# New operation lengths in the table of a planner that writes every queue

## The chip, the cores and the metric

The kernel runs on one core of one Trainium2 chip. The metric is device microseconds of one execution, from the launch on the device to its end. An execution taken by the profiler gives a span (the first instruction's start to the last one's end) and a time of its own a little above it.

## The reference, cut to what matters

Three stages follow each other. The arrays are float32, the feed-forward weights come as 64-bit floats that are converted on the chip.

```
# 1. attention, 2 batches x 8 heads x 768 positions x 64
bucket(z) = sum((z @ proj > 0) * 2**bit)          # 6 bits
scores = q @ k.T / 8, where bucket(q) == bucket(k), else -1e9
attn = softmax(scores); x = attn @ v              # x: 1536 tokens x 512

# 2. layer 1
h = x @ w_in                                      # 512 -> 2048
x = (h - tanh(h)) @ w_out                         # 2048 -> 512

# 3. layer 2
g = x @ w_gate                                    # 512 -> 1536
out = (g * sigmoid(g) * (x @ w_val)) @ w_out2     # 1536 -> 512
```

## The kernel before, in words

**Attention.** Heads go in pairs, 8 pairs in all, and each pair has 12 steps of 128 query rows (two halves of the sequence, two heads, three tiles). A step is: TensorE scores (L653), VectorE row maximum (L662), ScalarE exponential with row sum (L664), a reciprocal (L668, L670), GpSimd normalisation (L671), six transposes on TensorE (L682), a copy to SBUF (L688). After six steps come the products with the values (L706). For batch 0 GpSimd and ScalarE already split the result into the operands of layer 1 (`x_blocks`, L361 to L368).

**The layers.** Each number is split into a high and a low part, and a product takes three matmuls (high x high, high x low, low x high). The token blocks and the weights are combined after Strassen and Winograd: seven products (L850) instead of eight for a unit, whose sums VectorE forms (`add`, L833) from snapshots that ScalarE took (`snap`, L830). A unit is one of the matrices `in`, `gate` or `val`, 256 of its columns and one batch. Its results go through `block_tanh` (L791), `block_silu` (L798) or `block_val`, that is an activation on ScalarE and a `tt` (L779), and then through `split_g`: rounding on ScalarE (L784) and the remainder in `tt` (L779) again. Then `out_group` multiplies by the output weights (L904). In layer 1 the partial results are copied into a stage (L933) and added to `acc` by a DMA that accumulates, issued on GpSimd (L941), except the first, which is copied (L914, L915), and the last, which VectorE adds (L917). In layer 2 they are added to the output in HBM by such a DMA (L950), the last one by VectorE (L928).

**The weights.** A chunk of 64-bit floats is loaded on SP's queue (L271) into one of two `raw` buffers; three integer steps on VectorE (L273, L276, L279) make 32-bit floats of it in `fs` or `f`; subtractions (L305, L307) form the sums for the seven products, and `split_w` (L285 and L287) or its twin for the output weights (L322, L324) makes high and low parts in `wi` (two buffers) or `wo` (four).

**The planner.** Nothing of the order is written by hand. `op` records each operation with the engines that can do it, its length on each, the keys it reads and writes, a due time and the time `lat` from its end to the moment when others may use it (0.14 by default, 0.25 behind a matmul, some microseconds for a DMA). `Plan.order` then runs a simulation. Whenever an engine is free, it takes the operation with the lowest due time among those that are ready. An operation that names two engines goes to the one that reaches it first; on the second engine its due time is put back by `alt`. Operations that carry `port=BOTH` never overlap in the simulation, whichever of VectorE and GpSimd does them. Lengths of everything but TensorE's work declared behind the attention are multiplied by `SAFE`, 1.05. TensorE's due times are a clock that advances by the length of each product; all other due times are set off against it. The outcome is a list of (operation, engine), and each engine's queue is filled in that order and worked off in that order on the chip, each instruction waiting for its operands' semaphores. So the assumed lengths decide three things: the order in each queue, which engine does the operations that two can do, and when in the simulation a transfer is taken as landed. They don't change what an instruction does.

In the diff `W_TS` is the first integer step of a conversion, `W_STT` the two others; `pool(n)`, `dve(n)` and the new `act(n)` are the lengths of operations on n elements a partition; `TB` is 384 and `DM` 512. Some lengths of the attention are numbers of their own (0.87 for the maximum, 0.9 for the exponential, 0.95 for the normalisation). The split of batch 0 on GpSimd (`on_pool`) uses `pool(n)`.

Of the kernel before, what the change touches and what calls it, by code (L numbers as in the profile page):

```python
# [13 lines left out]
ACTF = mybir.ActivationFunctionType  # L14
# [171 lines left out]
def lsh_attention_moe_kernel(ctx: ExitStack, tc: tile.TileContext, qT, kT, vP, proj, cst, wts, out):  # L186
# [61 lines left out]
    W_TS, W_STT = 0.43, 0.69  # L248
# [3 lines left out]
    def pool(n):  # L252
        return 0.16 + n / 457

    def dve(n):
        return (n + 151) / 960 - 0.01
# [26 lines left out]
    def split_w(dst, src, rk, wk, n, due, late=False):  # L283
        hi, lo = dst
        op({"ACT": 0.19 + n / 1175}, lambda e: e.activation(out=hi, in_=src, func=ACTF.Copy),  # L285
# [32 lines left out]
    def declare_out(name, f, due, after):  # L318
# [3 lines left out]
        op({"ACT": 0.63}, lambda e: e.activation(out=hi, in_=f_t, func=ACTF.Copy),  # L322
# [455 lines left out]
    def tt(dst, dk, a, ak, b, bk, alu, due, port):  # L778
        op({"DVE": dve(TB), "POOL": pool(TB)} if port else {"DVE": 0.56}, lambda e: e.tensor_tensor(out=dst, in0=a, in1=b, op=alu),  # L779
           r=[ak, bk], w=dk, due=due, alt=ALT, port=BOTH * port)  # L780

    def split_g(key, src, sk, due, psum):
        (hi, hk, h1), (lo, lk, l1) = g_slot(), g_slot()
        op({"ACT": 0.52}, lambda g: g.activation(out=hi, in_=src, func=ACTF.Copy), r=[sk], w=[hk] + h1, due=due)  # L784
# [4 lines left out]
    def block_tanh(key, src, sk, due, psum, keep, spare=None):  # L789
        t, tk, t1 = spare or t_slot(1)  # L790
        op({"ACT": 0.51}, lambda e: e.activation(out=t, in_=src, func=ACTF.Tanh), r=[sk], w=[tk] + t1, due=due)  # L791
# [4 lines left out]
    def block_silu(key, src, sk, due, psum, keep, spare=None):  # L796
        t, tk, t1 = t_slot(2)
        op({"ACT": 0.51}, lambda e: e.activation(out=t, in_=src, func=ACTF.Sigmoid), r=[sk], w=[tk] + t1, due=due)  # L798
# [19 lines left out]
    def products(name, i, sb):  # L818
# [10 lines left out]
        def snap(dst, dk, bank, bk, due):  # L829
            op({"ACT": 0.49}, lambda e: e.activation(out=dst, in_=bank, func=ACTF.Copy), r=[bk], w=dk, due=due)  # L830

        def add(dst, dk, bank, bk, c, ck, due):
            op({"DVE": 0.56}, lambda e: e.tensor_tensor(out=dst, in0=bank, in1=c, op=ALU.add), r=[bk, ck], w=[dk], due=due)  # L833
# [48 lines left out]
    def out_group(layer, i, sb, j):  # L882
# [28 lines left out]
        if layer == 1 and i in (0, NP1 - 1):  # L911
            if i == 0:
                op({"DVE": dve(TB), "ACT": 0.5}, lambda g:
                   g.activation(out=acc_at(sb, j), in_=ps, func=ACTF.Copy) if g is nc.scalar else  # L914
                   g.tensor_copy(acc_at(sb, j), ps), r=[k], w=[("acc", sb, j)], due=e, late=True)  # L915
            else:
                op({"DVE": 0.57}, lambda g: g.tensor_tensor(  # L917
# [12 lines left out]
        else:  # L930
            at_, key, first = stage(layer, m)
            op({"ACT": 0.18 + size / 1200, "DVE": dve(size)}, lambda g, at_=at_:
# [4 lines left out]
            if m == n - 1:  # L937
                at_ = stages[layer, "at"]
                keys = [key[:3] + (c,) for c in range(n)]
                if layer == 1:  # L940
                    op({"POOL": 1.0}, lambda g, at_=at_: g.dma_start(out=acc_at(sb, 4 * t, 4), in_=at_(4), accum_op=ALU.add),  # L941
                       r=keys + aks, w=aks, due=e + 1, lat=5.0, late=True)
                else:
# [5 lines left out]
                    else:  # L949
                        op({"POOL": 1.0}, lambda g, at_=at_: g.dma_start(out=o, in_=src(at_), accum_op=ALU.add),  # L950
                           r=keys + [ok], w=[ok], due=e + 1, lat=5.0)
# [129 lines left out]
```

## Time and profile before

| what | value |
|---|---|
| median of 3 runs | 804.79 us (803.57 to 805.9) |
| the profiled execution | 803.86 us |
| its span | 802.1 us |
| instructions | 12309 |
| TensorE matmul, busy | 766.6 us, 96% |
| VectorE, busy | 589.4 us, 73% |
| ScalarE, busy | 466.8 us, 58% |
| GpSimd, busy | 359.7 us, 45% |

All times are microseconds unless ns is said. PE is TensorE's matmul, PEld its loading of weights, DVE is VectorE, ACT ScalarE, POOL GpSimd, SP the queue engine; L779 is line 779 of the kernel. A line says which engine does which operation, what it writes and reads (out<-in), the shapes, and x how many. An instruction's duration reaches from its start to the acknowledgement of its last write, and the next one on the same engine can start before that, so the sum of busy times counts such overlaps once. Matmul ends are modelled. The attention runs to about 264 us, layer 1 to about 532, layer 2 from there, overlapping at the seams.

### The profile page before, as it was taken

What the parts mean: (1) busy time and instruction counts of PE and PEld (TensorE: products, weight loads), DVE (VectorE), ACT (ScalarE), POOL (GpSimd) and SP (SyncE); (2) the same over time, 40 slices, a digit from 0 to 9 for tenths busy, and PEclk for the clock granted to TensorE, in tenths of its full rate; (3) what the DMA queues carried; (4) which work ended last, traced back from release to release, by engine and by line L of the source; (5) the groups of instructions that cost most, each with busy time, mean ns of one, the idle gap of its engine ahead of it and who ended that gap; (6) DMA issues with size and microseconds to landing.
All of it is one profiled execution on the core that took longest, in us unless ns stands there. A gap on an engine that the chain in (4) does not pass through costs nothing.

```text
span 802.1 us, 12309 instructions
## 1 busy us (share of the span) xinstructions
PE 766.6 (96%) x4332; PEld 661.5 (82%) x4332; DVE 589.4 (73%) x1038; ACT 466.8 (58%) x906; POOL 359.7 (45%) x384
## 2 busy tenths in 40 slices
PE   5999999999999999999999999989989999999997
PEld 3766666666668889999999999989979898989996
DVE  6877777787698966786777668777765876877444
ACT  4787787786666754666545545554544455555530
POOL 4655567744475341343323454735245532344121
PEclk9999999999999999999999999999999999999999
DMA  7655444553222143777776761324327567666675
GB/s 213 161 131 139 109 133 115 124 134 74 73 66 93 53 117 94 165 189 177 178 171 161 157 142 47 86 79 158 120 73 149 128 150 158 121 155 132 119 167 187
DMA packets 38717, 104.23 MB, mean 130 GB/s; under 512 B 4704, under 2 KB 10080, under 8 KB 38656
## 3 DMA queue, kind: packets, MB, share of 16 engines
q1 hardware_dynamic: 28288, 71.06, 29.0%
q0 software_dynamic: 9904, 31.59, 22.9%
q10 hardware_dynamic: 464, 0.80, 0.4%
q8 instruction: 34, 0.56, 0.3%
q14 instruction: 27, 0.22, 0.1%
HBM read 49.17 MB, written 18.87 MB: 85 GB/s over the span
## 4 chain that ended last, share of the span: by engine, by line
PE 76%; DVE 11%; DMA 4%; ACT 3%; issue 3%; POOL 2%; SPq 0%; DVEq 0%; ACTq 0%; POOLq 0%
PE s L850 26%; PE t L904 13%; PE x L706 7%; PE t L682 7%; PE s L653 7%; PE h L904 6%; PE x L904 4%; DMA raw<-in_w 3%; DVE m L662 2%; PE x L850 2%; PE t L850 1%; ACT ct L664 1%; DMA acc<-ct 1%; DVE ct L779 1%; DVE op L779 1%
## 5 line engine op out<-in xcount | busy, mean ns | idle before, releaser
L850 PE MATMUL s<-x,wi 128*128 128x384 f32 x1200 | 235.1, 337 | 6.4 <-DVE ct L833 2.1
L850 PEld LDWEIGHTS s<-x,wi 128*128 128x128 f32 x1200 | 209.1, 188 | 18.6 <-DVE ct L833 4.0
L662 DVE TENSOR_REDUCE m<-s 128x1 f32<-128x768 f32 x96 | 89.3, 951 | 29.3 <-PE s L653 28.7
L671 POOL TENSOR_SCALAR ct<-ct,r 128x768 f32<-128x768 f32 x96 | 94.1, 988 | 33.4 <-DVE r L670 29.2
L664 ACT ACTIVATE ct<-s,m 128x768 f32<-128x768 f32 x96 | 85.8, 896 | 20.6 <-DVE m L662 19.7
L653 PE MATMUL s<-op 128*128 128x384 f32 x384 | 88.9, 366 | 6.7 <-ACT ct L664 6.4
L830 ACT ACTIVATE ct<-s 128x384 f32<-128x384 f32 x120 | 58.1, 490 | 58.6 <-PE s L850 58.1
L682 PEld LDWEIGHTS t<-csb,ct 128*128 128x128 f32 x576 | 64.4, 141 | 31.2 <-issue 18.7
L682 PE MATMUL t<-csb,ct 128*128 128x128 f32 x576 | 81.6, 278 | 5.2 <-POOL ct L671 1.7
L904 PE MATMUL t<-op,wo 128*128 128x384 f32 x384 | 77.0, 338 | 4.8 <-DVE acc L917 1.5
L653 PEld LDWEIGHTS s<-op 128*128 128x128 f32 x384 | 66.5, 195 | 17.5 <-ACT ct L664 15.3
L904 PEld LDWEIGHTS t<-op,wo 128*128 128x128 f32 x384 | 66.9, 188 | 7.8 <-DVE acc L917 2.1
L706 PE MATMUL x<-pt,v 128*64 128x384 f32 x384 | 69.0, 495 | 0.0
L287 POOL TENSOR_TENSOR wi<-fs,wi 128x512 fp32r<-128x512 f32 (+1 forms) x37 | 57.1, 1553 | 24.1 <-ACT wi L285 18.0
L904 PE MATMUL t<-wo,op 128*128 128x512 f32 x264 | 67.5, 393 | 0.0
L688 ACT ACTIVATE pt<-t 128x768 f32<-128x768 f32 x59 | 47.9, 811 | 29.7 <-PE t L682 28.6
L324 POOL TENSOR_TENSOR wo<-f,wo 128x512 fp32r<-128x512 f32 x17 | 22.4, 1316 | 75.1 <-ACT wo L322 70.9
L904 PEld LDWEIGHTS t<-wo,op 128*128 128x128 f32 x264 | 48.9, 188 | 8.2
L850 PE MATMUL s<-op,wi 128*128 128x384 f32 x240 | 48.2, 337 | 1.8 <-DVE ct L779 1.6
L706 PEld LDWEIGHTS x<-pt,v 128*64 128x64 f32 x384 | 24.7, 136 | 28.4 <-issue 28.4
L285 ACT ACTIVATE wi<-fs 128x512 fp32r<-128x512 f32 (+1 forms) x60 | 41.5, 701 | 10.4 <-DVE fs L305 4.0
L779 POOL TENSOR_TENSOR ct<-ct 128x384 f32<-128x384 f32 x20 | 20.6, 1029 | 59.9 <-ACT ct L791 31.0
(164 smaller groups left out, 1378.8 us busy)
## 6 DMA issues: line engine op xcount, KB each, us to landing
raw<-in_w SPq DMA_DIRECT2D x68, 512.0 KB, 3.9
acc<-ct POOLq DMA_DIRECT2D x24, 768.0 KB, 6.0
out<-acc POOLq DMA_DIRECT2D x16, 768.0 KB, 7.8
op<-raw SPq DMA_DIRECT2D x42, 192.0 KB, 3.0
op<-f SPq DMA_DIRECT2D x56, 96.0 KB, 2.5
v<-in_v SPq DMA_DIRECT2D x8, 384.0 KB, 3.2
out<-acc SPq DMA_DIRECT2D x4, 768.0 KB, 4.1
acc<-out SPq DMA_DIRECT2D x4, 768.0 KB, 4.5
```

The costliest lines, as they stand in the source:

```text
L285: op({"ACT": 0.19 + n / 1175}, lambda e: e.activation(out=hi, in_=src, func=ACTF.Copy), r=rk, w=[wk + (0,)], due=due, late=late)
L287: op({"POOL": pool(n), "DVE": dve(n)}, lambda e: e.tensor_tensor(out=lo, in0=src, in1=hi.bitcast(F32), op=ALU.subtract), r=rk + [wk + (0,) ...
L653: g.matmul(out=s[:, kh, 0:TB], lhsT=(b, a)[first][:, q0], rhs=ks[kh][0 if first else 1], start=first, stop=not first,)
L662: op({"DVE": 0.87}, lambda g: g.tensor_reduce(out=m, in_=sv, axis=AX.XY, op=ALU.max, negate=True), r=[sk + (0,), sk + (1,)], w=[mk], due=d ...
L664: op({"ACT": 0.9}, lambda g: g.activation(out=p.rearrange("p (a b) -> p a b", a=2), in_=sv, func=ACTF.Exp, bias=m, accum_out=sm), r=[sk + ...
L671: op({"POOL": 0.95}, lambda g: g.tensor_scalar(out=p, in0=p, scalar1=r, scalar2=1.0, op0=ALU.mult, op1=ALU.mult), r=[pk, rk], w=[pk], due= ...
L682: g.transpose(out=t_t[0][:, kt // 3, c0:c0 + 128], in_=p[:, kt * 128:(kt + 1) * 128], identity=ident)
L688: op({"ACT": 0.75, "DVE": 0.87}, lambda g: g.activation(out=dst, in_=src, func=ACTF.Copy) if g is nc.scalar else g.tensor_copy(dst, src), ...
L706: g.matmul(out=x[r, :], lhsT=v[:, kt, r], rhs=pt_t[ptks[e][1]][:, kt, :], start=(kt == 0), stop=(kt == NKT - 1), tile_position=(0, 64 * e),)
L830: op({"ACT": 0.49}, lambda e: e.activation(out=dst, in_=bank, func=ACTF.Copy), r=[bk], w=dk, due=due)
L850: e.matmul(out=bank, lhsT=w[:, wpart, wi * 256 + k * 128:wi * 256 + k * 128 + 128], rhs=x_at(sb, xn, xpart, k), start=first and m == 0, st ...
L904: e.matmul(out=ps, lhsT=lhs, rhs=rhs, start=c == 0, stop=c == 5)
```

## The change

All lengths of the list below get new values; `act(n)` is a new function, and nothing else is different. The same formulas at 384 and 512 elements: `dve` 0.547 and 0.681 become 0.468 and 0.601, `pool` 1.000 and 1.280 become 0.970 and 1.250, the ScalarE lengths of 0.49 to 0.52 become 0.39 to 0.42 and 0.626 becomes 0.497. The accumulating DMA of layer 1 has an issue of 0.87 instead of 1.0 and lands 6.0 after it instead of 5.0; that of layer 2 1.3 and 7.5 instead of 1.0 and 5.0.

```diff
...
-    W_TS, W_STT = 0.43, 0.69
+    W_TS, W_STT = 0.34, 0.6
...
     def pool(n):
-        return 0.16 + n / 457
+        return 0.13 + n / 457
...
     def dve(n):
-        return (n + 151) / 960 - 0.01
+        return (n + 65) / 960
+
+    def act(n):
+        return 0.07 + n / 1200
...
     def convert(c, dst, dk, due, after, parts=1):
...
     def split_w(dst, src, rk, wk, n, due, late=False):
...
-        op({"ACT": 0.19 + n / 1175}, lambda e: e.activation(out=hi, in_=src, func=ACTF.Copy),
+        op({"ACT": act(n)}, lambda e: e.activation(out=hi, in_=src, func=ACTF.Copy),
...
-        op({"ACT": 0.63}, lambda e: e.activation(out=hi, in_=f_t, func=ACTF.Copy),
+        op({"ACT": act(512)}, lambda e: e.activation(out=hi, in_=f_t, func=ACTF.Copy),
...
     def tt(dst, dk, a, ak, b, bk, alu, due, port):
-        op({"DVE": dve(TB), "POOL": pool(TB)} if port else {"DVE": 0.56}, lambda e: e.tensor_tensor(out=dst, in0=a, in1=b, op=alu),
+        op({"DVE": dve(TB), "POOL": pool(TB)} if port else {"DVE": dve(TB) + 0.01}, lambda e: e.tensor_tensor(out=dst, in0=a, in1=b, op=alu),
...
     def split_g(key, src, sk, due, psum):
...
-        op({"ACT": 0.52}, lambda g: g.activation(out=hi, in_=src, func=ACTF.Copy), r=[sk], w=[hk] + h1, due=due)
+        op({"ACT": act(TB) + 0.03}, lambda g: g.activation(out=hi, in_=src, func=ACTF.Copy), r=[sk], w=[hk] + h1, due=due)
...
     def block_tanh(key, src, sk, due, psum, keep, spare=None):
...
-        op({"ACT": 0.51}, lambda e: e.activation(out=t, in_=src, func=ACTF.Tanh), r=[sk], w=[tk] + t1, due=due)
+        op({"ACT": act(TB) + 0.02}, lambda e: e.activation(out=t, in_=src, func=ACTF.Tanh), r=[sk], w=[tk] + t1, due=due)
...
     def block_silu(key, src, sk, due, psum, keep, spare=None):
...
-        op({"ACT": 0.51}, lambda e: e.activation(out=t, in_=src, func=ACTF.Sigmoid), r=[sk], w=[tk] + t1, due=due)
+        op({"ACT": act(TB) + 0.02}, lambda e: e.activation(out=t, in_=src, func=ACTF.Sigmoid), r=[sk], w=[tk] + t1, due=due)
...
         def snap(dst, dk, bank, bk, due):
-            op({"ACT": 0.49}, lambda e: e.activation(out=dst, in_=bank, func=ACTF.Copy), r=[bk], w=dk, due=due)
+            op({"ACT": act(TB)}, lambda e: e.activation(out=dst, in_=bank, func=ACTF.Copy), r=[bk], w=dk, due=due)
...
         def add(dst, dk, bank, bk, c, ck, due):
-            op({"DVE": 0.56}, lambda e: e.tensor_tensor(out=dst, in0=bank, in1=c, op=ALU.add), r=[bk, ck], w=[dk], due=due)
+            op({"DVE": dve(TB) + 0.01}, lambda e: e.tensor_tensor(out=dst, in0=bank, in1=c, op=ALU.add), r=[bk, ck], w=[dk], due=due)
...
         def product(n):
...
-                op({"DVE": dve(TB), "ACT": 0.5}, lambda g:
+                op({"DVE": dve(TB), "ACT": act(TB)}, lambda g:
...
-                op({"DVE": 0.57}, lambda g: g.tensor_tensor(
+                op({"DVE": dve(TB)}, lambda g: g.tensor_tensor(
...
-            op({"ACT": 0.18 + size / 1200, "DVE": dve(size)}, lambda g, at_=at_:
+            op({"ACT": act(size), "DVE": dve(size)}, lambda g, at_=at_:
...
-                    op({"POOL": 1.0}, lambda g, at_=at_: g.dma_start(out=acc_at(sb, 4 * t, 4), in_=at_(4), accum_op=ALU.add),
-                       r=keys + aks, w=aks, due=e + 1, lat=5.0, late=True)
+                    op({"POOL": 0.87}, lambda g, at_=at_: g.dma_start(out=acc_at(sb, 4 * t, 4), in_=at_(4), accum_op=ALU.add),
+                       r=keys + aks, w=aks, due=e + 1, lat=6.0, late=True)
...
-                        op({"POOL": 1.0}, lambda g, at_=at_: g.dma_start(out=o, in_=src(at_), accum_op=ALU.add),
-                           r=keys + [ok], w=[ok], due=e + 1, lat=5.0)
+                        op({"POOL": 1.3}, lambda g, at_=at_: g.dma_start(out=o, in_=src(at_), accum_op=ALU.add),
+                           r=keys + [ok], w=[ok], due=e + 1, lat=7.5)
```

## Rows read from the trace of the kernel before

**Rows 1.** The page's chain that ended last, shares of the span by engine.

```profile
PE 76%; DVE 11%; DMA 4%; ACT 3%; issue 3%; POOL 2%; SPq 0%; DVEq 0%; ACTq 0%; POOLq 0%
```

**Rows 2.** Busy us (x instructions) by stage: PE, PEld, DVE, ACT, POOL, clock, DMA share, GB/s.

```profile
264.00:300.00 36.00, 33.63 (x187) 31.88 (x186) 29.70 (x47) 23.09 (x46) 14.84 (x13) 1.00 0.29 75
300.00:460.00 160.00, 159.09 (x903) 155.95 (x903) 117.66 (x211) 89.73 (x190) 54.26 (x51) 1.00 0.68 162
460.00:532.00 72.00, 67.27 (x375) 64.36 (x374) 51.06 (x88) 38.05 (x72) 41.18 (x29) 1.00 0.37 87
532.00:640.00 108.00, 103.90 (x540) 95.09 (x540) 79.24 (x143) 52.56 (x103) 48.47 (x41) 1.00 0.45 125
640.00:782.00 142.00, 141.47 (x736) 130.07 (x735) 96.82 (x171) 71.60 (x139) 45.65 (x40) 1.00 0.68 142
250.00:802.00 552.00, 535.20 (x2883) 500.69 (x2881) 395.15 (x689) 284.72 (x570) 211.88 (x179) 1.00 0.56 134
```

**Rows 3.** PE's waits, 264 to 782 us: us in total, times, longest; twelve rows.

```profile
PE s L850 <- DVE op L779: 2.1, 3, 1.3
...
PE t L904 <- DVE acc L917: 1.5, 2, 1.1
...
PE s L850 <- DVE x L363: 0.2, 1, 0.2
```

**Rows 4.** VectorE's timeline in layer 1: start, duration, line, operation.

```profile
336.19 0.42 DVE L273 TENSOR_SCALAR fs<-raw 128x512 uint32<-128x512 uint32 x1
336.53 0.55 DVE L779 TENSOR_TENSOR op<-s,op 128x384 fp32r<-128x384 f32 x1
336.99 0.68 DVE L276 SCALAR_TENSOR_TENSOR f<-raw,f 128x512 uint32<-128x512 uint32 x1
337.59 0.68 DVE L276 SCALAR_TENSOR_TENSOR fs<-raw,fs 128x512 uint32<-128x512 uint32 x1
```

**Rows 5.** ScalarE's timeline at the passage to layer 2.

```profile
502.38 0.49 ACT L933 ACTIVATE ct<-x 128x384 f32<-128x384 f32 x1 [0.17 <-PE x L904]
502.76 0.49 ACT L791 ACTIVATE ct<-s 128x384 f32<-128x384 f32 x1
```

**Rows 6.** Groups on GpSimd, 250 to 802 us: busy us, mean ns, idle before.

```profile
L950 POOL DMA_DIRECT2D out<-acc x16 | 21.0, 1316 | 35.1 <-ACT acc L933 24.6 <-PE s L850 8.1 <-ACT op L784 2.4
L941 POOL DMA_DIRECT2D acc<-ct x24 | 21.0, 875 | 36.5 <-ACT op L784 11.7 <-ACT ct L933 10.8 <-DVE fs L279 5.8
L779 POOL TENSOR_TENSOR ct<-ct 128x384 f32<-128x384 f32 x20 | 20.6, 1029 | 59.9 <-ACT ct L791 31.0 <-ACT ct L798 26.5 <-DVE ct L833 2.4
```

**Rows 7.** The chain of waits in order of time, 490 to 626 us: start, duration, what.

```profile
498.08 6.72 DMA acc<-ct
...
525.00 0.50 ACT ct L830
525.53 0.58 DVE s L833
...
614.98 7.49 DMA raw<-in_w
```

**Rows 8.** The page's DMA issues: count, KB each, median us to landing.

```profile
acc<-ct POOLq DMA_DIRECT2D x24, 768.0 KB, 6.0
out<-acc POOLq DMA_DIRECT2D x16, 768.0 KB, 7.8
```

**Rows 9.** VectorE's timeline in layer 2, with the idle time before.

```profile
622.49 0.43 DVE L273 TENSOR_SCALAR fs<-raw 128x512 uint32<-128x512 uint32 x1 [3.55 <-DMA raw<-in_w]
```

**Rows 10.** Groups by line and shape on GpSimd in the attention, 25 to 216 us.

```profile
L363 POOL TENSOR_TENSOR x<-ct,x 128x384 fp32r<-128x384 f32 x14 | 14.0, 1002 | 4.1 <-ACT x L361 4.1
...
L368 POOL TENSOR_TENSOR ct<-ct 128x384 f32<-128x384 f32 x8 | 8.1, 1012 | 0.2
```

**Rows 11.** The timeline of all engines around 512 us.

```profile
511.78 2.29 POOL L363 TENSOR_TENSOR op<-acc,op 128x768 fp32r<-128x768 f32 x1
...
512.29 2.06 DVE L273 TENSOR_SCALAR f<-raw 128x512 uint32<-128x512 uint32 x1
```

## The prediction, made before the changed kernel ran

> **What bounds the kernel now.** I read the chain of waits first. Three quarters of the span hang on TensorE and a tenth on VectorE [rows 1]: the end is set by TensorE's own work plus the moments when it stands. So I went to the busy time by stage. After the attention, TensorE is busy 33.63 of 36.00 us, 159.09 of 160.00, 67.27 of 72.00, 103.90 of 108.00 and 141.47 of 142.00 [rows 2]. The differences are 2.4, 0.9, 4.7, 4.1 and 0.5, together 12.6 us between 264 and 782 us. The reader is to see that in the long steady stretches of both layers TensorE never stands; what it loses lies at the start of layer 1, at the passage to layer 2 and in the first fifth of layer 2. VectorE, ScalarE and GpSimd are busy 395, 285 and 212 of 552 us there, so none is a bound by volume. The list of TensorE's waits in that stretch has twelve groups, 21 waits, from 2.1 us down to 0.2 [rows 3]; the large ones are on VectorE. Its clock is at 1.00, the 2.4 GHz level, in every stage, so the clock has no part in it.
>
> TensorE's work itself is untouched by the change, so about 12.6 us is the whole sum that a better order behind the attention can give, and the profiled execution (803.86 us, its span 802.1 with 1.8 around it) is what I count from. The median of the runs shown is 804.79, 0.9 above it.
>
> **What the change edits.** No instruction, size or transfer of the computation is added or removed. The planner simulates the engines and writes down the order of every queue and, for an operation that two engines can do, which one does it. The edit alters only the lengths that it assumes. Are the new ones nearer to the chip?
>
> VectorE: the operation behind a 384-wide one starts 0.46 us after it although that one lasts 0.55 (336.53 to 336.99) [rows 4]. Old length 0.547 (the `dve` formula at 384) or 0.56, new 0.468 or 0.478. The two integer steps of the weight conversion have 0.34 and 0.60 to the next start while lasting 0.42 and 0.68 [rows 4]; old 0.43 and 0.69, new 0.34 and 0.60. ScalarE: 0.38 apart, lasting 0.49 [rows 5]; old 0.49 to 0.52, new 0.39 to 0.42. GpSimd's length falls by 0.03 everywhere. So the old lengths were durations and the new ones are distances, right within 0.01 us; the planner multiplies both by 1.05.
>
> One rule speaks against this. The Trainium skill, "VectorE: DVE Perf Modes", section The DRAIN you can't avoid, says that the next operation does not start until the pipe of the one before it is empty, which would make the duration the distance. By it each VectorE operation would come 0.55 - 0.49 = 0.06 us later than planned, three in a chain, before 21 waits: 3.8 us slower, 807.7. The trace disagrees: the next start lies 0.08 to 0.09 us before the end [rows 4], and the measurement decides.
>
> *What it sums to in the planner.* 689 VectorE operations behind 250 us [rows 2] times 0.083 (0.079 x 1.05) is 57 us less booked in 552; 570 ScalarE operations times some 0.11 is 63 us less. None of this is time of the chip: the operations take what they took. It acts in two ways.
>
> (1) Who does the shared operations. GpSimd does 179 instructions in that stretch [rows 2], of which 24 and 16 issue accumulating DMAs [rows 6]; the other 139 are operations that VectorE could do. One of them takes 1.03 us on GpSimd [rows 6] against 0.55 on VectorE, so each that lies in a chain on which TensorE waits gives back about 0.5 us. VectorE looks 57 us freer to the planner, so it will take some: I take 30 of the 139 (57 us would hold 120 at 0.47; most are taken by whichever engine is free first, and GpSimd stays free half of the time). In chains that end in a TensorE wait I expect one in five of these: 6 x 0.5 = 3 us.
>
> (2) The order on TensorE, VectorE and ScalarE. A step which the planner believes late is placed later than need be; with truer lengths the two layer boundaries (2.4 + 4.7 us of standing) should be packed a little better. But a longer assumed length is also a cushion. The dependent chain of one block is six operations, three on ScalarE and three on VectorE (snapshot, add, tanh, subtract, rounding, remainder): 3 x 0.105 + 3 x 0.083 = 0.56 us less cushion per chain. Is there any left? From the chain: the ScalarE step of 0.50 us from 525.00, and 0.03 later VectorE's, of 0.58 [rows 7]: 0.53 and some 0.61 from start to start. The planner now says 0.39 x 1.05 + 0.14 = 0.55 and 0.478 x 1.05 + 0.14 = 0.64. Both still cover the rows by 0.03, so nothing undisturbed arrives late. Bounds for the whole of (1) and (2): all 12.6 us gone below; above, all 21 waits longer by 0.56, 11.8 us. The value that I take is a third of the standing at the boundaries and in the first part of layer 2, (2.4 + 4.7 + 4.1) / 3 = 3.7 us, which contains the 3 us of (1); nearest to the rows that show undisturbed chains still covered.
>
> **The DMA edits.** Accumulating into `acc` lands after 6.0 us (old 5, new 6), accumulating into `out` after 7.8 (old 5, new 7.5) [rows 8], and their issues hold GpSimd for 0.88 and 1.32 us [rows 6] (old 1.0 both, new 0.87 and 1.3). Nobody is queued behind them long: the only TensorE chain with a landing of `acc` in it is the one at the passage to layer 2, where it stands with 6.72 us from 498.08 [rows 7]. Gain between 0 and 1.1 us, the longest of TensorE's waits on `acc` [rows 3]; I take 0, as it is in the third above. The weight stream's landing stays at 3.5 us in the planner, and one load took 7.49 [rows 7]; VectorE stood 3.55 us before its conversion [rows 9]. The change does not mend this, and those waits stay.
>
> **The attention.** Its lengths stay, except that the 384-wide GpSimd operations that split its result go from 1.00 to 0.97; there are 22 of them, lasting 1.00 to 1.01 [rows 10]. It shifts the simulated clock of GpSimd by 0.03 at a time and can swap neighbours. Bounds -2 and +2 us: two of these of a microsecond swapped either way in the final stretch, where the weights of layer 1 are already being converted. I take 0, since these rows fit either length.
>
> Sum: 803.86 - 3.7 = 800.2 from the profiled execution; the median lies 0.9 above, 801.1. I say 801.
>
> **Rivals.** *A, no change (804.8, the median as it is).* TensorE's order is fixed by due times whenever its operands are ready, and in 302 us of steady stretches they are ready [rows 2]. If the waits at the boundaries come from the dependence itself, with the products of the first block needing the split of a whole half, other lengths only shift them. For it: the waits are spread over twelve small groups. Against: the shared operations will really change hands. That the edit does nothing to the order at all would end here as well; with some 120 us of booked time changed that is unlikely.
>
> *B, slower (about 809).* Collisions of VectorE and GpSimd. Place: VectorE's queue where GpSimd works at its side. A conversion step that takes 0.42 us took 2.06, ending 0.3 us behind GpSimd's 2.29 us subtraction [rows 11]: the one stood until the other was through. The planner keeps the two apart by booking their shared port for the planned length, so the surplus of 0.08 us behind each VectorE operation was a guard against the chip running off the plan. With only 5% left, any lateness (a weight load at 7.49 for 3.5 us) puts operations side by side. Price: 2.06 - 0.42 = 1.6 us each. It decides the sign when more than 3.7 / 1.6, that is three, new collisions fall into chains that TensorE waits for; four of them with half of the gain lost give 804.8 - 1.9 + 6.4 = 809.3, six give 812.5. For it: the waits stand where GpSimd is busiest, 41 of 72 us at the passage [rows 2]. Against: fewer operations on GpSimd mean fewer partners to collide with. The Trainium skill, "SBUF — State Buffer", Who interferes with whom, states the same as a rule: a VectorE operation that uses the port pair it shares with GpSimd (two inputs in SBUF, or a 2-port mode) and a GpSimd one exclude each other for a whole instruction. By it, a planner that misjudges starts pays whole operations, as in this rival; the trace agrees with its 2.06.
>
> *C, much faster (about 796).* Two thirds of the standing goes, 8.4 us from 804.8, because the passage to layer 2 is mended by the 6.0 us landing. For it: one wait of that passage hangs on `acc`; against: the rest there do not.
>
> **How the numbers follow.** Chances: forecast 0.41, C 0.07, A 0.27, B 0.25. About 0.3%, 2.4 us, is what a measurement of this kernel can tell from no change; faster means below 802.4, slower above 807.2. The forecast's own range is 797 to 803.5, a little of it within no change, which A's upper edge gives back: faster 0.47, same 0.29, slower 0.24. Range: 795 takes in two thirds of C, and 810 takes in B up to four collisions; left out are a third of C and about half of B, 0.15 together. The bounds of (1) and (2), 12.6 either way, lie beyond both ends and are reached only if every wait goes or grows.
>
> **What would show it.** Right: GpSimd's instructions behind 250 us fall from 179 by some 30 and VectorE's 689 rise by as many; TensorE's waits from 264 to 782 us sum to about 9 us, with the passage from 460 to 532 below 4; the attention ends within 2 us of 264. The steady stretches stay at under 1 us each. Rival B: new VectorE operations of two microseconds beside GpSimd ones, and TensorE waits on VectorE above 12.6. The prediction is wrong if the attention's end moves by more than 2 us, since I gave that nothing, or if the steady stretches begin to show waits.

## The result, and the profile after

The changed kernel took 810.55 us (median of 4 runs, 810.01 to 811.53) beside 804.18 of the kernel before on the same chip: a ratio of 1.0080, 95% interval 1.0056 to 1.0105. It is slower by 6.4 us, where 801.0 was predicted. Its profiled execution took 810.85, with a span of 809.1. In its code, lines behind L259 are numbered 3 higher: L850 is L853, L779 L782, L830 L833, L833 L836, L784 L787, L904 L907.

The distances that the change copied into the planner are still those of the chip. VectorE's timeline in layer 1 answers to [rows 4]:

```profile
342.32 0.55 DVE L836 TENSOR_TENSOR ct<-s,ct 128x384 f32<-128x384 f32 x1
342.78 0.68 DVE L279 SCALAR_TENSOR_TENSOR f<-raw,f 128x512 uint32<-128x512 uint32 x1
...
343.94 0.42 DVE L276 TENSOR_SCALAR fs<-raw 128x512 uint32<-128x512 uint32 x1
344.27 0.68 DVE L282 SCALAR_TENSOR_TENSOR f<-raw,f 128x512 uint32<-128x512 uint32 x1
344.87 0.56 DVE L836 TENSOR_TENSOR t<-t,ct 128x384 f32<-128x384 f32 x1
```

A 384-wide operation is followed after 0.46 us, the integer steps after 0.33 and 0.60. So the new table describes these distances better, and the kernel is slower. The landings of the accumulating DMAs, which the table now has at 6.0 and 7.5, did not move either [rows 8]:

```profile
acc<-ct POOLq DMA_DIRECT2D x24, 768.0 KB, 6.0
out<-acc POOLq DMA_DIRECT2D x16, 768.0 KB, 7.7
```

The busy time by stage answers to [rows 2], with the same columns:

```profile
264.00:300.00 36.00, 34.30 (x190) 31.06 (x188) 28.22 (x45) 23.77 (x48) 18.14 (x15) 1.00 0.24 67
300.00:460.00 160.00, 158.13 (x890) 153.44 (x889) 117.79 (x214) 88.21 (x189) 43.66 (x43) 1.00 0.68 162
460.00:532.00 72.00, 69.98 (x392) 67.24 (x390) 57.77 (x95) 40.00 (x76) 37.02 (x28) 1.00 0.41 99
532.00:640.00 108.00, 102.28 (x525) 92.56 (x526) 84.03 (x148) 55.96 (x109) 36.08 (x32) 1.00 0.45 129
640.00:782.00 142.00, 139.51 (x722) 127.52 (x721) 92.81 (x168) 71.11 (x138) 38.77 (x31) 1.00 0.61 123
...
250.00:809.00 559.00, 540.34 (x2895) 502.00 (x2893) 408.06 (x713) 288.91 (x578) 176.74 (x149) 1.00 0.54 131
```

GpSimd has 149 instructions behind 250 us where it had 179, and VectorE 713 where it had 689; GpSimd's loss of 30 is the predicted number, but it is a balance (see the steps of the prediction below). TensorE stands 1.7, 1.9, 2.0, 5.7 and 2.5 us in the stages, together 13.8 where it was 12.6. The passage and the start of layer 2 improved a little (7.7 for 8.8), the steady stretches of both layers got worse (4.4 for 1.4). Two waits head the list from 264 to 782 us, in the columns of [rows 3], and both are steps of a block on a bank of `s`:

```profile
PE s L853 <- ACT op L787: 3.9, 4, 1.4
PE s L853 <- DVE ct L782: 2.5, 4, 0.9
```

The first, on ScalarE's rounding, is new. The second stood in the list before with 1.9:

```profile
PE s L850 <- DVE ct L779: 1.9, 4, 0.7
```

Busy time hides part of the standing, which the prediction did not see. A matmul's end is modelled: a 384-wide one is drawn 0.33 us long, while the next can start 0.173 us after it, so a pause of 0.1 us between two of them still counts as busy. Starts show it: two 384-wide matmuls in a row start 0.173 us apart, 512-wide ones 0.231. What goes beyond that from 270 us to the end, counting pauses over 0.03 us, adds up to 22.4 us in 77 pauses before and 25.4 in 101 after. I use this sum below.

### The profile page after: what moved, and what is told of

It reads as the page before. It is cut to its first block, busy times and chain, and to the rows that moved or that the text cites. A ratio compares the mean times of both kernels' runs of the same rounds, so it can differ in the third digit from the quotient of the medians.

```text
span 809.1 us, 12324 instructions
## 1 busy us (share of the span) xinstructions
PE 770.0 (95%) x4332; PEld 661.1 (82%) x4332; DVE 602.7 (74%) x1067; ACT 468.5 (58%) x911; POOL 322.2 (40%) x350
## 5 line engine op out<-in xcount | busy, mean ns | idle before, releaser
L853 PE MATMUL s<-x,wi 128*128 128x384 f32 x1200 | 236.2, 338 | 7.9 <-ACT op L787 3.9
L853 PEld LDWEIGHTS s<-x,wi 128*128 128x128 f32 x1200 | 208.9, 188 | 21.4 <-ACT op L787 7.7
L674 POOL TENSOR_SCALAR ct<-ct,r 128x768 f32<-128x768 f32 x96 | 92.2, 968 | 32.5 <-DVE r L673 28.5
L667 ACT ACTIVATE ct<-s,m 128x768 f32<-128x768 f32 x96 | 85.9, 897 | 22.9 <-DVE m L665 16.4
L833 ACT ACTIVATE ct<-s 128x384 f32<-128x384 f32 x120 | 58.9, 491 | 48.8 <-PE s L853 46.3
L907 PE MATMUL t<-op,wo 128*128 128x384 f32 x384 | 78.1, 339 | 3.9 <-DVE op L782 1.6
L907 PEld LDWEIGHTS t<-op,wo 128*128 128x128 f32 x384 | 66.6, 188 | 8.5 <-DVE op L782 2.9
L907 PE MATMUL t<-wo,op 128*128 128x512 f32 x264 | 67.8, 393 | 0.0
L691 ACT ACTIVATE pt<-t 128x768 f32<-128x768 f32 x57 | 46.2, 811 | 28.9 <-PE t L685 27.8
L290 POOL TENSOR_TENSOR wi<-fs,wi 128x512 fp32r<-128x512 f32 (+1 forms) x26 | 40.3, 1552 | 46.3 <-ACT wi L288 46.3
L907 PEld LDWEIGHTS t<-wo,op 128*128 128x128 f32 x264 | 48.9, 187 | 7.9
L782 POOL TENSOR_TENSOR ct<-ct 128x384 f32<-128x384 f32 x19 | 20.0, 1052 | 86.2 <-ACT ct L801 47.8
L853 PE MATMUL s<-op,wi 128*128 128x384 f32 x240 | 48.4, 336 | 1.3 <-DVE ct L782 1.0
L944 POOL DMA_DIRECT2D acc<-ct x24 | 21.0, 877 | 67.4 <-ACT ct L936 38.2
```

The costliest lines, as they stand in the source:

```text
L290: op({"POOL": pool(n), "DVE": dve(n)}, lambda e: e.tensor_tensor(out=lo, in0=src, in1=hi.bitcast(F32), op=ALU.subtract), r=rk + [wk + (0,) ...
L667: op({"ACT": 0.9}, lambda g: g.activation(out=p.rearrange("p (a b) -> p a b", a=2), in_=sv, func=ACTF.Exp, bias=m, accum_out=sm), r=[sk + ...
L674: op({"POOL": 0.95}, lambda g: g.tensor_scalar(out=p, in0=p, scalar1=r, scalar2=1.0, op0=ALU.mult, op1=ALU.mult), r=[pk, rk], w=[pk], due= ...
L691: op({"ACT": 0.75, "DVE": 0.87}, lambda g: g.activation(out=dst, in_=src, func=ACTF.Copy) if g is nc.scalar else g.tensor_copy(dst, src), ...
L833: op({"ACT": act(TB)}, lambda e: e.activation(out=dst, in_=bank, func=ACTF.Copy), r=[bk], w=dk, due=due)
L853: e.matmul(out=bank, lhsT=w[:, wpart, wi * 256 + k * 128:wi * 256 + k * 128 + 128], rhs=x_at(sb, xn, xpart, k), start=first and m == 0, st ...
```

## What stood behind the late steps

The largest single wait of that new group, in the timeline of the changed kernel (start, duration, engine, line, operation, and the idle time before with what ended it):

```profile
528.59 2.24 PE L853 MATMUL s<-x,wi 128*128 128x384 f32 x12
...
529.39 0.48 ACT L833 ACTIVATE ct<-s 128x384 f32<-128x384 f32 x1
530.93 0.57 DVE L836 TENSOR_TENSOR s<-s,ct 128x384 f32<-128x384 f32 x1 [1.41 <-PE s L853]
531.54 0.57 DVE L782 TENSOR_TENSOR s<-s,ct 128x384 f32<-128x384 f32 x1
532.14 0.56 DVE L836 TENSOR_TENSOR ct<-s,ct 128x384 f32<-128x384 f32 x1
532.73 0.49 ACT L787 ACTIVATE op<-s 128x384 fp32r<-128x384 f32 x1 [2.86 <-DVE ct L836]
533.27 1.34 PE L853 MATMUL s<-x,wi 128*128 128x384 f32 x6 [1.40 <-ACT op L787]
```

The first row is two products. VectorE's `add` needs the first, which ends at 529.79, and ScalarE's snapshot, through at 529.87. It starts at 530.93, behind the second product (through at 530.83), whose result goes to the other bank of the same tile `s` and is none of its operands. Four steps later TensorE stands for 1.40 us.

`s` is two tiles and `t` one, each of two PSUM banks ([128, 2, 512] float32); `x` and `h` are tiles of one bank. The program's waits are kept by tile: an operation on one bank waits for whatever another engine does on the other bank, if that stands earlier in the program. The planner's keys are single banks, so it does not know these waits. I compared each operation of VectorE and ScalarE behind 264 us with the end of its operands and of its predecessor. Before, 61 start more than 0.3 us late, 65.2 us in all, and 53 of them (60.3 us) end with a matmul on the sibling bank; after, 32 of 41 (37.3 of 43.5 us). The typical one costs 1.08 us, about one product (six matmuls, 1.04 us from start to start). Of TensorE's own standing 7.0 of 12.7 us before and 7.5 of 13.7 after end with an operation on the sibling bank. By the sum of late starts the changed kernel waits less (43.5 us for 65.2), and yet it is slower: what such a wait costs depends on whether TensorE comes to stand behind it, which the sum does not tell.

## The experiments

Texts on record speak of theories by number or letter. *1*: with shorter lengths, a block's chain of dependent steps has less cushion. *1b* (later *H*): the old surplus stood in for time that engines are held by waits which the planner does not know. *2*: who does the shared operations, or the engine's booking, matters. *3* (later *R*): any other order costs a few us by chance. *W*: the waits between banks are the cost. *T*: the attention's end, which comes later, is what is left of the loss. All ratios are to the kernel before on the same chip; differences between runs that stood on different chips are taken from the ratios, at 803.3 us.

**Parts of the change, and the cushion.** On the changed kernel, a chain latency of 0.23 behind the attention; on the kernel before, 0.05:

```diff
-        self.ops.append((eng, fn, deps, due, self.LAT if lat is None else lat, late, after,
+        self.ops.append((eng, fn, deps, due, (self.LAT if not self.n_first else 0.23) if lat is None else lat, late, after,
```

> The changed kernel, with one more edit: behind the attention the planner takes a result as usable 0.23 us after the operation's end instead of 0.14, so a chain of dependent operations is as long in the plan as before the change (0.083 to 0.105 us an operation), while the engines are still booked by the new distances. Theory 1 (the old lengths held a cushion for results that come later than planned, and the change took it away): most of the 6.4 us comes back, 804 to 807 us, and TensorE's waits from 300 to 782 us fall to those of before. Theory 2 (what counts is how long the engines are booked, and through it who does the shared operations): no change from the changed kernel, 810 to 811. Theory 3 (any reshuffling of these queues moves the time by some us, without a rule): anywhere from 803 to 813.

> The kernel before with 0.05 instead of 0.14 us from an operation's end to its use, behind the attention: chains as short in the plan as after the change, engines booked as long as before. Theory 1b: 802 to 806 us. Theory 1: 808 to 812. Theory 3: 804 to 817.

Measured: 809.16 us, 1.0081 (1.0065 to 1.0096), and 806.81, 1.0044 (1.0030 to 1.0058). Giving the chain its 0.09 us a step back mends nothing; taking as much from the kernel before costs 3.5 us.

Then the kernel before with only VectorE's lines of the diff, only ScalarE's, only those of the accumulating DMAs, and those with `pool(n)`:

> The kernel before with VectorE's new lengths alone (dve(n), the two conversion lengths and the fixed VectorE lengths). Theory 1: about half of the chain's cushion is gone (3 of 6 operations), so about half of the loss: 806 to 808 us. Theory 2: nearly the whole loss, 809 to 811, since this part alone lets VectorE take the shared operations from GpSimd. Theory 3: 803 to 813.

> The kernel before with ScalarE's new lengths alone. Theory 1: the other half of the loss, 806 to 808 us. Theory 2: no loss, 804 us, since ScalarE shares few operations with GpSimd. Theory 3: 803 to 813.

> The kernel before with the new issue lengths and landings of the accumulating DMAs alone. It moves 144 operations to another engine and changes the order of as many pairs on VectorE as ScalarE's new lengths alone did (about 600), without making an engine's work shorter. Theory 1b: 802 to 806 us, as before. Theory 3: as b_act, 809 to 817.

> The kernel before with GpSimd's length shorter by 0.03 and the new issue lengths and landings of the accumulating DMAs, nothing else. Theories 1 and 2: the time of before within 0.3%, 802 to 806.5 us, since neither a cushion nor a share moves. Theory 3: the queues are reshuffled here too, so 801 to 810, and if it comes out over 807 the loss has no rule that the lengths explain.

Measured: 817.69, 1.0184 (1.0166 to 1.0202); 813.35, 1.0129 (1.0114 to 1.0144); 806.86, 1.0045 (1.0029 to 1.0061); 803.41, 1.0000 (0.9989 to 1.0012). Shorter lengths of either engine alone cost more than both together, so the parts don't add; an order that is new without shorter lengths on these engines costs 0 or 3.6 us.

Then the changed kernel with its lengths on VectorE and ScalarE booked longer than by 1.05:

```diff
-        eng = {e: t * (1 if e == "PE" or not self.n_first else self.SAFE) for e, t in eng.items()}
+        eng = {e: t * (1 if e == "PE" or not self.n_first else 1.2 if e in ("DVE", "ACT") else self.SAFE) for e, t in eng.items()}
```

> The same with 1.12, half way. Theory 1b: between the two, 805 to 809 us. Theory 3: no order in the three factors; 803 to 817.

> The changed kernel with the lengths of VectorE and ScalarE behind the attention multiplied by 1.20 instead of 1.05: the new table, but engines booked about as long as before the change (384-wide: 0.56 on VectorE, 0.47 on ScalarE). After the first four runs theory 1 is restated as 1b: the booked length stands in for time in which an engine is blocked by waits that the planner doesn't know, not for the latency of a chain. Theory 1b: 802 to 806 us. Theory 1 (latency of a chain): 802 to 806 too. Theory 3 (any reshuffling of the tuned queues costs): about 810, within 804 to 817.

Measured: at 1.12 812.83, 1.0124 (1.0101 to 1.0147); at 1.20 803.60, 1.0006 (0.9992 to 1.0020). At 1.20 the old surplus is back and so is the old time. It is no smooth curve: 1.12 is worse than 1.05, where theory 1b expected 805 to 809; theory 3, that the order of the three factors says nothing, had this right.

**The waits between banks taken out.** The order stays, instruction for instruction; operations on different banks of `s` or `t` are declared independent when they are issued, unless they also share an operand:

```diff
+    def emit(n, e):
+        made.clear()
+        plan.ops[n][1](eng[e])
+        mine = plan.touch[n]
...
+                    for n2, e2, both, i2 in seen.get(other, []):
+                        if e2 != e and not both and n2 not in plan.ops[n][2]:
+                            for i in made:
+                                tc.declare_no_dep(i.ins, i2, reason="another bank")
...
-            plan.ops[n][1](eng[e])
+            emit(n, e)
```

> The changed kernel, in its own order, instruction for instruction, but an operation on one PSUM bank of the tiles s and t no longer waits for a matmul or an operation on the other bank of the same tile (no data pass between the two banks; every wait on the operation's own bank stays). In the trace of the changed kernel 32 of 41 late starts of VectorE and ScalarE behind 264 us (37.3 of 43.5 us) end with such a matmul, and 17 of 27 standings of TensorE (7.5 of 13.7 us) with such an operation. Theory H (the old lengths were too long by about as much as these waits hold the engines up, so they stood in for waits that the planner does not know, and the true lengths are too short only because of them): with the waits gone the true lengths are enough, 797 to 803 us, and no slower than the kernel before with the same waits taken out. Theory R (any other order of some thousand operations costs a few us by chance): it gains at most the 7.5 us of TensorE's standing, to 803 to 810, and stays about 6 us behind the kernel before with the waits taken out.

> The kernel before, in its own order, with the same waits between the two banks of s and t taken out: its trace has 53 of 61 late starts of VectorE and ScalarE behind 264 us (60.3 of 65.2 us) and 15 of 24 standings of TensorE (7.0 of 12.7 us) that end with them. Theory H: the old lengths already leave room for these waits, so most of the 60 us cost nothing and only TensorE's own standing goes, 797 to 803 us, equal to or above the changed kernel without the waits. Theory R: the same 7 us, 797 to 799, and the changed kernel without the waits about 6 us above it.

Measured: the changed kernel 786.78, 0.9795 (0.9782 to 0.9809); the kernel before 785.21, 0.9776 (0.9762 to 0.9789). By the ratios the waits cost 18.0 us in the old order and 22.9 in the new one, and of 6.4 us between the two kernels 1.6 are left (785.21 and 786.78 stood on one chip). R's numbers are false for these two orders, since it gave at most 7.5 us back and left 6. H is right on where the loss lies, wrong on the sign of the rest, and its 797 to 803 us missed both: the old lengths did not make these waits free, they still cost 18.0 us.

The rest has two parts, told apart by the last twelve products with the values in the attention:

```profile
261.99 2.16 PE L706 MATMUL x<-pt,v 128*64 128x384 f32 x12
```

```profile
264.53 2.16 PE L709 MATMUL x<-pt,v 128*64 128x384 f32 x12
```

They start 2.5 us later in the changed kernel, and 3.2 later with the waits out of both. From there to the end the changed order takes 4.5 us more than the old one with the waits (544.5 and 540.1), and 1.8 us less without them (520.8 and 522.6). So what the waits account for is the loss behind the attention; the later end of the attention is a loss of its own. Behind the attention H's sign holds, in one execution of each.

The place at 528.59 us again, in the changed kernel without the waits (every row has the recording line L1029 here):

```profile
515.95 2.24 PE L1029 MATMUL s<-x,wi 128*128 128x384 f32 x12
...
516.75 0.48 ACT L1029 ACTIVATE ct<-s 128x384 f32<-128x384 f32 x1
517.26 1.17 DVE L1029 TENSOR_TENSOR s<-s,ct 128x384 f32<-128x384 f32 x2 [0.26 <-ACT ct L1029]
...
518.46 0.49 ACT L1029 ACTIVATE op<-s 128x384 fp32r<-128x384 f32 x1 [1.23 <-DVE s L1029]
```

The `add` comes 0.03 us behind the snapshot, in the middle of the second product, and the rounding 2.51 us after the products' start instead of 4.14. TensorE's waits from 264 to 766 us, the changed kernel's first, then the kernel before's:

```profile
PE s L1029 <- DVE ct L1029: 2.1, 3, 0.9
```

```profile
PE s L1026 <- DVE ct L1026: 3.6, 4, 1.3
PE x L1026 <- DVE op L1026: 0.2, 1, 0.2
```

And the steady stretch of layer 1 in the two, PE alone, to be read against x903 before and x890 after:

```profile
300.00:460.00 160.00, 159.93 (x923) 1.00 0.71 167
```

```profile
300.00:460.00 160.00, 159.83 (x922) 1.00 0.69 164
```

Before, this stretch was 159.09 of 160.00 busy and looked full; 19 more matmuls fit into it. The pauses by starts are 3.6 us in 12 (changed) and 5.4 in 12 (before), from 25.4 and 22.4.

**The planner told of the waits.** The program keeps them; an operation on `s` or `t` is planned only when what other engines have under way on the tile is done:

```diff
+        def blocked(n, e, now):
+            return n >= self.n_first and any(
+                e2 != e and t > now + 1e-9 for k in self.touch[n] for e2, t in busy.get(k, {}).items())
```

> The changed lengths; the program keeps its waits, but the planner now knows them: behind the attention part an operation on a tile of two PSUM banks is planned to start only once what other engines have under way on that tile is done. The order is new. Theory H: the true lengths with the true waits give an order that runs as planned, at or below the kernel before, 797 to 805 us, and clearly below the 810.6 of the changed kernel. Theory R: one more order among many, 803 to 818 us like the orders run so far, with no reason to lie below 804.

> The old, too long lengths, and the planner knows the waits between the two banks of a tile as in the run on the changed lengths. Theory H: the waits are now booked twice, once by the rule and once in the lengths, so the plan leaves TensorE and GpSimd idle time that the chip does not need: 803 to 810 us, behind the changed lengths with the same rule. Theory R: one more order, 803 to 818 us, with equal odds to lie ahead of or behind the changed lengths with the rule.

> The waits stay, the planner knows them, and VectorE's and ScalarE's new lengths are booked times 1.20. With the true lengths this rule gave 805.3, with the old lengths 795.5. If a cushion beside the rule is what the true lengths lack, 794 to 798 like the old lengths; if 795.5 was a lucky order, 799 to 808.

Measured: new lengths 805.30, 1.0024 (1.0015 to 1.0033); old lengths 795.50, 0.9901 (0.9886 to 0.9916); new lengths times 1.20 794.62, 0.9888 (0.9875 to 0.9902). H said the reverse: with the waits known, the true lengths should have been the best. They are 10 us behind the longer ones, so in these orders the surplus is worth something beside the waits. The longest wait in the trace of the new lengths with the rule:

```profile
529.60 2.28 POOL L382 TENSOR_TENSOR acc<-acc 128x768 f32<-128x768 f32 x1
530.12 2.05 DVE L287 TENSOR_SCALAR fs<-raw 128x512 uint32<-128x512 uint32 x1
...
531.84 1.99 POOL L377 TENSOR_TENSOR x<-acc,x 128x768 fp32r<-128x768 f32 x1
532.09 2.29 DVE L293 SCALAR_TENSOR_TENSOR fs<-raw,fs 128x512 uint32<-128x512 uint32 x1
534.30 0.55 DVE L847 TENSOR_TENSOR s<-s,ct 128x384 f32<-128x384 f32 x1
...
536.61 0.56 DVE L793 TENSOR_TENSOR op<-s,op 128x384 fp32r<-128x384 f32 x1
...
537.22 2.29 PE L864 MATMUL s<-x,wi 128*128 128x384 f32 x6 [5.57 <-DVE op L793]
```

This is rival B's mechanism, at the passage to layer 2: beside GpSimd's 768-wide operations two conversion steps take 2.05 and 2.29 us instead of 0.42 and 0.68, the chain behind them is late, and TensorE stands for 5.57 us. The planner books the two engines apart, so here one has run off the plan against the other. But this place does not explain the 10 us. The wait is 5.57 of them at most. As much again is lost in layer 1, where this order has 884 matmuls from 300 to 460 us and the old lengths with the rule 918 (34 of 0.173 us). And meetings of VectorE and GpSimd are as frequent in the faster orders: VectorE operations over 0.15 us longer than their form's usual time are 35 here, 36 with the old lengths and 34 with the factor 1.20, whose order has a wait of 3.8 us at the passage too.

**The other orders without the waits.**

> The order of VectorE's new lengths alone (817.7 us, the slowest so far), instruction for instruction, without the waits between the two banks of s and t. If these waits are what makes orders differ (W), the 15 us go with them and it lands with the other two, 785 to 788, the upper end by the attention part that ends 2.2 us late in this order too. If the order itself is bad (R), it gains what the other two gained, 18 to 24 us, and stays at 794 to 800.

> The changed lengths with a chain latency of 0.23 behind the attention part (809.2 us), without the waits between banks. Its attention part ends about 3 us earlier than that of the changed kernel. If the 1.6 us that the changed kernel keeps on the kernel before without the waits are that end (T), this one lands 2 to 3 us under it: 783.5 to 785. If they are worse lengths behind the attention part, it stays at 786 to 788.

> VectorE's and ScalarE's new lengths times 1.20 behind the attention part (803.6 us, the best of the orders with the waits), without the waits between banks. If longer booking is worth something only as a stand-in for these waits (W), nothing of its lead of 7 us on the changed kernel is left but the end of the attention part: 783.5 to 786. If cushions are worth something by themselves, it leads by more: 778 to 782.

Measured: 793.92, 0.9886 (0.9871 to 0.9900); 789.61, 0.9834 (0.9819 to 0.9848); 784.70, 0.9762 (0.9744 to 0.9781). The order booked at 1.20 keeps 2.7 of its lead of 5.9 us, inside W's range. By the ratios the slowest order gained 23.9 us, but stayed 8.8 above the kernel before without the waits: W's number was missed, and R's, a gain of 18 to 24 and a time of 794 to 800, was met but for 0.1. So over five orders run both ways the waits cost 18.0 us (the kernel before), 19.6 (1.20), 19.8 (latency 0.23), 22.9 (the changed kernel) and 23.9 (VectorE's lengths alone). The slower orders lose more by them, but they are not the whole difference between orders: of the 14.8 us of the slowest 8.8 stay without them, and 4.7 of the 6.5 of the order with 0.23.

What is left in the slowest one is mainly two places. From the products with the values at 227 us to the last ones of the attention it takes 38.1 us, where the kernel before takes 34.8, and at the passage it has one wait that none of the fast ones has:

```profile
PE h L1026 <- DVE op L1026: 5.3, 1, 5.3
```

The order with latency 0.23 ends its attention 1.0 us ahead by the same count (33.8 us), and loses more than that at the same passage, with a wait of 3.9 us; it lies above both of the numbers that it was to decide between. In both traces two conversion steps ahead of the wait are longer by 1.6 us each beside 768-wide operations on GpSimd, as in the trace of the section before.

**One operation of the attention's end.** By the same count the changed kernel takes 37.1 us instead of 34.8, and 36.8 without the waits. It is on time at 227 us and 2 us late in the next twelve products. VectorE's lengths alone end the attention later too (38.1), ScalarE's as well (36.5), but both are on time in those products and fall behind after them. GpSimd of the changed kernel there:

```profile
229.24 1.84 POOL L290 TENSOR_TENSOR wi<-fs,wi 128x768 fp32r<-128x768 f32 x1
...
231.73 2.51 POOL L290 TENSOR_TENSOR wi<-fs,wi 128x512 fp32r<-128x512 f32 x2
234.20 0.91 POOL L674 TENSOR_SCALAR ct<-ct,r 128x768 f32<-128x768 f32 x1
...
238.99 2.16 PE L709 MATMUL x<-pt,v 128*64 128x384 f32 x12
```

and in the kernel before:

```profile
229.83 2.62 POOL L671 TENSOR_SCALAR ct<-ct,r 128x768 f32<-128x768 f32 x2
229.85 0.94 DVE L287 TENSOR_TENSOR wi<-fs,wi 128x768 fp32r<-128x768 f32 x1
232.43 2.68 POOL L287 TENSOR_TENSOR wi<-fs,wi 128x512 fp32r<-128x512 f32 x2
...
236.88 2.16 PE L706 MATMUL x<-pt,v 128*64 128x384 f32 x12
```

Three remainders of weights stand ahead of the normalisations that TensorE waits for. I handed the 768-wide one back to VectorE, in both versions of the changed kernel:

```diff
+    order = [(n, "DVE" if n == 1209 else e, t) for n, e, t in order]
```

> The changed kernel with one operation handed back: the 768-wide remainder at 229.24 us (1.84 us on GpSimd) is issued to VectorE (0.94 us in the trace of before) at the same place of the order; every other instruction stands where it stood. If this operation makes the end of the attention late (T), its last products come about 2 us earlier and the time falls to 808 to 809. If GpSimd's queue is late for another reason, it stays within 0.5 us of 810.6.

> The same edit on the changed kernel without the waits between banks (786.8 us). T: 784 to 785, level with the kernel before without these waits (785.2) or below it, since behind the attention it loses 1.8 us less. Otherwise 786 to 787.5.

Measured: 810.67, 1.0092 (1.0077 to 1.0107), and 785.53, 0.9775 (0.9761 to 0.9788). The first refutes the expectation that this one operation makes the end late: the attention takes 36.7 us, 1.9 more than before instead of 2.3, while the two 512-wide remainders still stand ahead of the normalisations. The second lies between T's number and the other. That the rest of the lateness comes from the order of these two is read from the rows and was not tried.

## Why the prediction was wrong, by its steps

- *"Both still cover the rows by 0.03, so nothing undisturbed arrives late"* is the step that failed. It held one undisturbed chain against the new lengths. But 53 of the 61 late starts in the same trace ended with a matmul on the other bank of a tile, not with an operand or the engine's own work, and the prediction has no term for such waits. Taking them out shows what they do: they cost 18.0 us in the old order and 22.9 in the new one, a difference of 4.9 out of 6.4. That the old table's surplus had hidden this part is argued, not shown: it booked 57 and 63 us too much on VectorE and ScalarE, 120 together and twice the 60.3 us that these waits take from the two; booking the surplus again (1.20) gave the old time back, but 1.12 did not, and with the waits known to the planner the longer lengths were still the better ones. Why shorter lengths led to an order that exposes TensorE more to these waits stays open.
- *A third of the standing goes, 3.7 us*: the sign came out the other way. Behind 270 us the changed order pauses 3.0 us more than the old one; only where both are without these waits does it pause less, by 1.8.
- *"About 12.6 us is the whole sum"*, and TensorE never stands in the steady stretches: both wrong. The same order without the waits is 18.0 us faster, and the stretch from 300 to 460 us takes 19 more matmuls. The rows counted as busy the pauses under drawn ends.
- *(1) Thirty operations change hands*: 30 is what GpSimd lost on balance, and that the number agrees is luck. In the planner's two lists 168 operations declared behind the attention have another engine: 72 go from GpSimd to VectorE, 43 from VectorE to GpSimd, and 53 change between VectorE and ScalarE. The 3 us for it are not to be found.
- *The DMA edits, 0*: with GpSimd's edit 0, alone 3.6 us slower. The landings in that run, 6.3 and 7.9 us, are no shorter than before, so what the edit changed is the order; where the 3.6 us lie in it was not followed.
- *The attention, 0, bounds 2 either way*: its last products start 2.5 us later, beyond the bounds. The prediction named the place (weights of layer 1 beside the final stretch) and put the term at 0 because the rows of 384-wide operations fit either length; what moved ahead of the normalisations were remainders of 768 and 512 elements.
- *The rule against the change, 807.7*: the sentence of the Trainium skill, "VectorE: DVE Perf Modes", The DRAIN you can't avoid, has an exception beside it that the prediction leaves out, an operation that is not held starts earlier. So the starts 0.08 to 0.09 us before the end [rows 4] do not contradict the page.
- *Rival B* had the sign, but not its mechanism: VectorE's operations over 0.15 us longer than their form's usual time fell from 31 to 25 behind 264 us, and those over 1 us are 5 in both. That its 809 lies near the 810.55 is luck. Meetings of VectorE and GpSimd have a part in single long waits at the passage in other orders, and there its price of 1.6 us each held. The Trainium skill, "SBUF — State Buffer", Who interferes with whom, has VectorE and GpSimd exclude each other for a whole instruction on operations that use the port pair they share; the rows of 2.05 and 2.29 us agree.

What stays open: what the surplus is worth beside the waits, why 1.12 is worse than 1.05, what sets the 4.7 and 8.8 us by which two orders differ from the old one without the waits, and the two remainders at the attention's end. That another order of these queues differs by some us without a rule (R) is not excluded.

The fastest versions are all without the waits: the new lengths times 1.20 (784.70), the kernel before (785.21) and the changed kernel with the one operation handed back (785.53). Their intervals overlap, and each beats both kernels by over 2%.

## What to carry to other kernels

Before making a planner's lengths truer, list the starts in the trace that neither an operand nor the engine's own queue explains: they point at waits that the planner cannot see, and these were worth more here (18.0 and 22.9 us) than the lengths (6.4). Declare the banks of a PSUM tile independent where engines work on both at once; a tile for each bank should do the same, which was not tried. Judge how full TensorE is by matmuls in a window, not by its busy share.

## What was not expected of the hardware

Nothing that these runs show of the chip asks for the waits between banks: without them matmuls wrote one bank of a tile while VectorE and ScalarE worked on the other, at unchanged durations (`add` and `tt` as a pair of 1.17 us above, 0.57 each in the changed kernel; operations that write `s` from `s` take 0.56 us on average in all six kernels run so). The Trainium skill, "PSUM — Partial Sum Buffer", PSUM bank collisions raise a hardware error, asks for semaphores by bank; the program's were by tile.

The longest waits cost more than themselves. TensorE stood for 5.57 us, and the next six matmuls took 2.29 us instead of 1.21 (the row at 537.22 above). The granted clock is 0.69 over the 9 us that follow, 0.50 in the first four of them, which is the 1.2 GHz level, and 1.00 again from 543 us:

```profile
530.00:537.00 7.00, 1.65 (x10) 0.91 0.21 68
537.00:546.00 9.00, 8.78 (x32) 0.69 0.20 64
```

Behind the 5.3 us of the slowest order without the waits it is 0.70 over 9 us, behind the 3.9 us of the order with 0.23 it is 0.81, and behind the longest wait of the kernel before, 1.5 us, it stays at 1.00.
